# Attention and a token and channel mixer on one core: new durations and waits in the planner that sets the order

## The chip, the cores and the metric

The kernel runs on one core of a Trainium2 chip. The metric is the device time of one launch in microseconds (us); lower is better. TensorE (PE) multiplies matrices, with its weight loads shown apart as PEld; VectorE (DVE), ScalarE (ACT) and GpSimd (POOL) do the elementwise work, and SyncE (SP) issues the DMA transfers.

## The reference, cut to what matters

```python
def _attn_ref(q, k, v):                       # 8 x 8 heads, 576 rows, 64 columns
    scores = (1.0 / np.sqrt(D)) * np.matmul(q, k.transpose(0, 1, 3, 2))
    mask = pos[:, None] // 64 >= pos[None, :] // 64
    scores = np.where(mask, scores, -1000000000.0)
    attn = np.exp(scores - np.max(scores, axis=-1, keepdims=True))
    attn = attn / (np.sum(attn, axis=-1, keepdims=True) + 1e-09)
    return np.matmul(attn, v).astype(np.float32)

def _moe_ref(x, U, V, w_ch1, w_ch2):          # x: 8 x 576 x 512, the heads side by side
    h = x.transpose(0, 2, 1) @ U @ V          # U 576 x 32, V 32 x 576
    u = x + h.transpose(0, 2, 1)
    ch = np.maximum(u @ w_ch1, 0.0) @ w_ch2   # w_ch1 512 x 2048, w_ch2 2048 x 512
    return (u + ch).astype(np.float32)
```

The four matrices arrive as 64 bit words, and the kernel makes single precision numbers of them itself.

## The kernel before, in words

The work is cut into some 6500 tasks, each on one engine. `add(engine, ns, prio, fn, reads, writes, ...)` writes down a task with the nanoseconds that it is taken to occupy its engine, a priority (lower goes first) and the buffers that it reads and writes. `Plan.issue` then runs a list schedule in the build: each engine, when it is free by these nanoseconds, takes the ready task of the lowest priority number, and `fn` writes its instructions down. So the durations are never waited for on the chip. They set only the order of each engine's instructions, which the chip then executes strictly in that order, each one waiting on semaphores for what it needs. Buffers of a pool (PSUM banks) are handed out in that same run.

Three tables hold the waits between engines. After a task ends, `TAIL[e]` passes before its result leaves engine `e`, and `INTO[x]` more before a task on engine `x` can use it; `NEAR` is the wait on the same engine and `DL` that of a transfer. DVE tasks marked `port=True` and all POOL tasks are never planned at the same time.

```python
TAIL = {"PE": 165, "DVE": 78, "ACT": 105, "POOL": 20, "SP": 0}
INTO = {"PE": 355, "DVE": 35, "ACT": 35, "POOL": 310, "SP": 60}
```

The stages, in the order of time in the profile:

- Attention, 64 heads, to about 700 us. For a head: scores (L1185 for the first 12 heads, L1189 and L1190 after), maxima `mx` on DVE (L1203), exponentials `p` on ACT (L1214), reciprocals `rv` on DVE (L1230, L1231), normalising on POOL (L1240), transposes on PE (L1273), copies to `ph` on ACT (L1250) and the remainder `pl` on DVE (L1292, L1299), the product with V (L1316 for the first 10 heads, L1332 after), its two halves joined over `tmp` on ACT (L1338) and `xt` on DVE (L1340). After each second head `mix` multiplies with U and V (PE L1358, L1372, L1387; ACT L1361 `xh`, L1375 `tb`, L1377; DVE L1363 `xl`, L1376 `tz`, L1392 `ut`).
- Preparing the channel matrices beside it. A block of 128 x 512 numbers is fetched into `st` and made single precision: ACT L359, POOL L362, DVE L338, L343 and L351 (which writes `wr`), then its largest value by DVE L387. When a set of blocks is there, `power` finds a power of two (DVE L397, PE L401, DVE L407, PE L421, DVE L423), and each block is split in a high and a low half of 16 bits, ACT L455 and DVE L459. There are four such sets for the first half of the hidden width: `w1` block 0, `w2` block 0, `w1` block 1, `w2` block 1. With the last goes `agree` (DVE L482 to L488, tile `joint`), after which `level` multiplies the first four rows of `w2` again (four ACT instructions, L499).
- The first half of the channel mixer, `ffn_chunk`, in 16 chunks of 288 tokens: up products (PE L631), ACT L636 and DVE L639, down products (PE L656), DVE L668. Their PE tasks have the highest priority numbers (1e6 and up), so that PE takes them when nothing of the attention is ready. Tasks of chunks 0 and 1 come in two turns, since the second `w1` and `w2` blocks arrive late: until the second `w2` block is split, PE has only the up products of the second turn.
- The blocks of the second half of `w1` are prepared in the same manner at priority 9e5, below everything of the attention, and those of `w2` after it.
- From 834 us on, the second half of the hidden width, by a seven product scheme (PE L873).

PE, DVE, ACT and POOL each see one queue. What stands ahead in a queue and waits holds back what is behind it, whatever its priority.

Of the kernel before, what the change touches and what calls it, by code (L numbers as in the profile page):

```python
# [34 lines left out]

STAGES1 = (
# [17 lines left out]
INTO = {"PE": 355, "DVE": 35, "ACT": 35, "POOL": 310, "SP": 60}  # L54
# [86 lines left out]
class Plan:  # L141
# [105 lines left out]
def _dve(n):  # L247
    return 69 + 1.042 * n
# [13 lines left out]
def attention_then_mixer(  # L262
# [60 lines left out]
    def split64(fetches, shape, hi, lo, dst, prio, gate=(), part=slice(None), whole=None):  # L323
# [32 lines left out]
        if len(shape) > 2:  # L356
# [4 lines left out]
            "POOL", 250 + 0.85 * n, prio,  # L361
# [3 lines left out]
        add("DVE", 130 + 0.55 * n, prio, shift, [st, zt], [zt], port=True)  # L365
        add("DVE", 100 + 1.15 * n, prio, put_upper, [st, zt], [zt], port=True)
# [23 lines left out]
    def power(mu, n, by, sc, prio, pool):  # L390
# [5 lines left out]
            "DVE", 150, prio,  # L396
# [39 lines left out]
    def weights_of(half_bufs, hi, lo, blocks, scale, prio, limit=None):  # L436
# [15 lines left out]
        for n, b in enumerate(half_bufs["out"]):  # L452
            add(
                "ACT", _act(CW, True) + 90, last,
                lambda n=n: nc.scalar.activation(hi(n), raw[:, n, :], AF.Copy, scale=scale[:, 0:1]), [x[n], scale], [b],  # L455
            )
            add(
                "DVE", 150 + 1.3 * CW, last,
                lambda n=n: nc.vector.scalar_tensor_tensor(  # L459
                    out=lo(n), in0=raw[:, n, :], scalar=scale[:, 0:1], in1=hi(n), op0=ALU.mult, op1=ALU.subtract  # L460
                ),
                [x[n], scale, b], [b], port=True,
            )
# [10 lines left out]
    def agree(prio):  # L474
# [15 lines left out]
        add("DVE", 500, prio, limits, [a, b, c], [d, joint])  # L490
        add("DVE", 200, prio, ratio, [a, b, c, d], [joint])

    def level(w, bufs):

        for x in ("w2h", "w2l"):
            for k in range(0, FH, 2):
                add(
                    "ACT", _act(2 * CW, True), -1.0,
                    lambda x=x, k=k: nc.scalar.activation(w()[x][:, k : k + 2, :], w()[x][:, k : k + 2, :], AF.Copy, scale=joint[:, 0:1]),  # L499
                    [joint], bufs["w2"][k : k + 2],  # L500
                )
# [76 lines left out]
    def ffn_chunk(c, w, wb, fr=range(FC), turn=0):  # L578
# [12 lines left out]
        for k in range(KC):  # L591
            uh, ul = uh_r[k], ul_r[k]
            if not b:
                add(
                    "ACT", _act(T, True), E,
# [3 lines left out]
                    "DVE", _dve(T), E,  # L599
# [5 lines left out]
            else:  # L605
                us = take(us_r, "us")
                add(
                    "POOL", 250 + 0.85 * T, E,
# [6 lines left out]
                add("POOL", 780, E, lambda us=us, h=uh, l=ul: nc.gpsimd.tensor_sub(l.ap, us.ap, h.ap), [us, uh], [ul])  # L615
# [64 lines left out]
    def block_products():  # L680
# [115 lines left out]
        def piece(x, sc):  # L796
# [3 lines left out]
            if sc is None:  # L800
# [28 lines left out]
        def copied(out, x, iv=None):  # L829
            if iv is None:  # L830
# [3 lines left out]
                "ACT", _act(2 * T), E, lambda: nc.scalar.activation(out[0](), x[0](), AF.Copy, scale=iv.ap), [x[1], iv], [out[1]]  # L834
# [325 lines left out]
    def softmax(h, tiles, pr):  # L1160
# [37 lines left out]
        else:  # L1198
            add("PE", _pe(*ns, m=ms) + 40, pr, products, [q1, k1, q2, k2], [bank])
# [24 lines left out]
    def normalise(h, tiles, pr):  # L1224
# [9 lines left out]
        for i in tiles:  # L1234
# [4 lines left out]
                "POOL", 250 + 0.85 * w, pr,  # L1239
# [12 lines left out]
    def transpose(h, g, part, pr):  # L1252
# [41 lines left out]
        if m < n:  # L1294
# [3 lines left out]
                "DVE", _dve(64), pr,  # L1298
# [3 lines left out]
    def apply_v(h, g, pr):  # L1302
# [6 lines left out]
        if h < FP:  # L1309
# [11 lines left out]
            add("PE", cost + 15, pr, whole_products, [vr, *pt.parts], [bank], hold=[xb])  # L1321
# [15 lines left out]
        add("PE", cost + 80, pr, products, [vs, *ph.parts, *pl.parts], [bank], hold=[xb, tmp])  # L1337
        add("ACT", _act(n), pr, lambda: nc.scalar.copy(tmp[0:64, :n], bank[64:P, :n]), [bank], [tmp])  # L1338
# [5 lines left out]
    def mix(p, pr):  # L1344
# [3 lines left out]
        for rows, js in ((P, range(4)), (64, range(4, 5))):  # L1348
# [6 lines left out]
            def products(view=view, js=js, rows=rows):  # L1355
# [7 lines left out]
                "DVE", _dve(n * P), pr, lambda hi=hi, lo=lo, view=view: nc.vector.tensor_sub(lo, view(), f32(hi)),  # L1363
# [11 lines left out]
        add("ACT", _act(P), pr, lambda: nc.scalar.copy(tb.ap, low[R : 2 * R, 0:P]), [bank], [tb])  # L1375
        add("DVE", _dve(P), pr, lambda: nc.vector.tensor_add(tz.ap, low[0:R, 0:P], tb.ap), [bank, tb], [tz])  # L1376
# [126 lines left out]
```

## Time and profile before

| what | value |
|---|---|
| three runs | 1168.57, 1167.81, 1168.48 us; median 1168.48 |
| the profiled execution | 1168.67 us, of which the span from the first to the last instruction is 1166.9 us |
| busy share of the span | PE 97%, PEld 80%, DVE 82%, ACT 68%, POOL 45% |
| granted clock of PE, mean | 0.993 |
| chain that ended last | PE 70%, DVE 13%, ACT 12%, issue 3% |

The page of the profile gives the busy time of each engine, then the span in 40 equal slices with a digit for the busy tenths of each engine and the granted clock of PE, the groups of instructions by line, and the chain of work that ended last. A row of a timeline has its start, its length, the engine, the line and the tiles, and behind it in brackets the idle time before it and the instruction that ended it. A view of stretches gives the busy time of each engine between two times, with the count of its instructions.

### The profile page before, as it was taken

How to read it: one execution, taken by the hardware profiler on the slowest of the kernel's cores; microseconds unless marked ns; L12 is line 12 of the kernel's file. 1: busy time of each engine (PE TensorE's matmuls, PEld its weight loads, DVE VectorE, ACT ScalarE, POOL GpSimd, SP SyncE). 2: the span in 40 equal slices, each digit the busy share in tenths (PEclk: the TensorE clock that was granted, in tenths of full speed). 3: DMA queues.
4: the chain of work that ended last, by engine and by line, in shares of the span. 5: the costliest groups of instructions: out<-in, count | busy, mean ns of one | idle time of the engine just before them, and what ended most of it. 6: DMA issues, size and time to landing. Idle time of an engine off the chain costs nothing.

```text
span 1166.9 us, 25406 instructions
## 1 busy us (share of the span) xinstructions
PE 1135.2 (97%) x9044; PEld 934.4 (80%) x9044; DVE 958.3 (82%) x2129; ACT 794.0 (68%) x1936; POOL 524.2 (45%) x696
## 2 busy tenths in 40 slices
PE   9999997999999999999999999999999999999998
PEld 7777776877888888888888887777777777777777
DVE  6899998889887878787878773372599999999998
ACT  7878887887898888888788954325345455554543
POOL 5445554876767685858576736737200000000000
PEclk9999997999999999999999999999999999999999
DMA  5454552735443434434433312241303422331321
GB/s 142 135 146 128 152 165 83 210 114 145 119 125 103 116 105 118 110 105 114 115 101 102 94 47 72 88 134 51 102 32 92 122 62 62 122 112 34 101 82 41
DMA packets 75885, 122.70 MB, mean 105 GB/s; under 512 B 8944, under 2 KB 52976, under 8 KB 75760
## 3 DMA queue, kind: packets, MB, share of 16 engines
q1 hardware_dynamic: 75760, 121.09, 36.4%
q8 instruction: 71, 1.16, 0.4%
q14 instruction: 54, 0.44, 0.1%
HBM read 76.23 MB, written 29.49 MB: 91 GB/s over the span
## 4 chain that ended last, share of the span: by engine, by line
PE 70%; DVE 13%; ACT 12%; issue 3%; POOL 1%; DMA 0%; SPq 0%; ACTq 0%; DVEq 0%; POOLq 0%
PE bb L873 28%; PE bf L656 9%; PE bf L631 8%; PE ba L1273 5%; ACT p L1214 5%; PE ba L1332 4%; PE bg L656 3%; PE bg L631 3%; DVE mx L1203 3%; DVE pl L1292 2%; PE ba L1316 2%; PE ba L1189 1%; ACT ph L1250 1%; PE ba L1190 1%; DVE xt L1340 1%
## 5 line engine op out<-in xcount | busy, mean ns | idle before, releaser
L1240 POOL TENSOR_SCALAR p<-p,rv 128x576 f32<-128x576 f32 (+4 forms) x320 | 170.6, 548 | 125.9 <-DVE rv L1231 91.6
L1273 PE MATMUL ba<-ident,p 128*128 128x128 f32 x768 | 123.1, 276 | 7.0 <-ACT p L1214 2.2
L1214 ACT ACTIVATE p<-ba,mx 128x448 f32<-128x448 f32 (+3 forms) x248 | 114.5, 465 | 22.3 <-DVE mx L1203 17.7
L1292 DVE TENSOR_TENSOR pl<-ba,ph 128x512 fp32r<-128x512 f32 x216 | 113.7, 550 | 14.8 <-ACT ph L1250 12.6
L656 PEld LDWEIGHTS <-w2h 128*128 128x128 f16 x1024 | 100.5, 98 | 29.7 <-issue 3.7
L873 PE MATMUL bb<-hh,w1l 128*128 128x288 f16 x448 | 118.9, 286 | 0.0
L873 PE MATMUL bb<-hh,w2h 128*128 128x288 f16 x448 | 118.9, 286 | 0.0
L873 PE MATMUL bb<-hh,w2l 128*128 128x288 f16 x448 | 118.9, 286 | 0.0
L873 PE MATMUL bb<-hh,w1h 128*128 128x288 f16 x448 | 118.9, 286 | 0.0
L656 PE MATMUL bf<-hh,w2h 128*128 128x288 f16 x408 | 118.2, 290 | 0.4 <-DVE ot L668 0.4
L631 PEld LDWEIGHTS <-w1h 128*128 128x128 f16 x1024 | 97.6, 98 | 25.5 <-issue 1.7
L656 PE MATMUL bf<-hl,w2h 128*128 128x288 f16 x408 | 117.3, 288 | 0.0
L656 PE MATMUL bf<-hh,w2l 128*128 128x288 f16 x408 | 117.3, 288 | 0.0
L801 ACT CAST hh<-hb 128x576 f16<-128x576 f32 x96 | 63.6, 666 | 66.8 <-DVE hb L827 43.0
L873 PEld LDWEIGHTS <-w1h 128*128 128x128 f16 x896 | 87.7, 98 | 22.0
L873 PEld LDWEIGHTS <-w2h 128*128 128x128 f16 x896 | 87.7, 98 | 22.0
L1250 ACT CAST ph<-ba 128x512 fp32r<-128x512 f32 x216 | 98.6, 493 | 9.6 <-PE ba L1273 8.1
L1273 PEld LDWEIGHTS ba<-ident,p 128*128 128x128 f32 x768 | 90.1, 142 | 13.7 <-issue 7.8
L1203 DVE TENSOR_REDUCE mx<-ba 128x1 f32<-128x448 f32 (+3 forms) x248 | 94.1, 405 | 4.7 <-PE ba L1190 3.2
L1332 PE MATMUL ba<-ph,vs 128*128 128x256 f32 (+3 forms) x432 | 93.2, 272 | 1.8 <-DVE pl L1292 1.5
L873 PE MATMUL bb<-hl,w2h 128*128 128x288 f16 x448 | 91.6, 286 | 0.0
L873 PE MATMUL bb<-hl,w1h 128*128 128x288 f16 x448 | 91.6, 286 | 0.0
(193 smaller groups left out, 3197.0 us busy)
## 6 DMA issues: line engine op xcount, KB each, us to landing
raw<-in_qk_dram SPq DMA_DIRECT2D x63, 288.0 KB, 3.9
st<-in_w_dram SPq DMA_DIRECT2D x32, 512.0 KB, 3.8
o_d<-ot SPq DMA_DIRECT2D x72, 144.0 KB, 1.8
vr<-in_v_dram SPq DMA_DIRECT2D x32, 320.0 KB, 3.8
ur<-u_d SPq DMA_DIRECT2D x64, 144.0 KB, 2.5
wr<-o_d SPq DMA_DIRECT2D x32, 288.0 KB, 3.1
out_dram<-wr SPq DMA_DIRECT2D x31, 288.0 KB, 2.3
ur<-u_d SPq DMA_DIRECT2D x30, 288.0 KB, 3.2
```

The costliest lines, as they stand in the source:

```text
L631: nc.tensor.matmul(ps[:, :T], w()[wn][:, k, fs], m[k].ap, start=(i == 0), stop=(i == len(ops) - 1))
L656: nc.tensor.matmul(ps[:, :T], w()[wn][:, f, ms], hs[f][x].ap, start=(i == 0), stop=(i == len(ops) - 1))
L801: add("ACT", _act(2 * T, True), E, lambda: nc.scalar.copy(h.ap, x[0]()), [x[1]], [h])
L873: nc.tensor.matmul(bank[:, i, :T], x()[:, w(k)], p.ap[:, k, :], start=first and n == 0, stop=last and n == len(ops) - 1)
L1203: lambda i=i, at=at: nc.vector.tensor_reduce(out=mx[: P if i else 64, i : i + 1], in_=view(i, at), op=ALU.max, axis=AX.XY if wide else AX. ...
L1214: nc.scalar.activation(out.rearrange("p (j k) -> p j k", j=2) if wide else out, view(i, at), AF.Exp, bias=mx[:rows, i : i + 1], accum_out= ...
L1240: lambda x=x, rows=rows, i=i: nc.gpsimd.tensor_scalar(out=x, in0=x, scalar1=rv[:rows, i : i + 1], scalar2=1.0, op0=ALU.mult, op1=ALU.mult),
L1250: add("ACT", _act(n), pr, lambda: nc.scalar.copy(out(), inp()), reads, writes)
L1273: nc.tensor.transpose(out=bank[:, a : a + P], in_=pt_r[i][h % PB[i]][:, j * P : (j + 1) * P], identity=perm.ap)
L1292: "DVE", _dve(m), pr, lambda: nc.vector.tensor_sub(pl[:, low], bank[:, :m], f32(ph[:, low])), [bank, bh], [bl]
L1316: nc.tensor.matmul(bank[:, a:n], vr[:, x : x + 2, :], pt[:, _at(g, j)], start=(j == 0), stop=(j == NK[g] - 1))
L1332: nc.tensor.matmul(bank[0 : c.stop, a:n], vs[:, j, c], x[:, _at(g, j)], start=(i == 0), stop=(i == len(ops) - 1))
```

## The change

Durations in the calls of `add` and the table `INTO` are replaced, and each duration is multiplied by a factor between 0.98 and 1.02 that depends on the task's number. No task is added or removed, and no priority, buffer or dependency is changed. What each instruction computes stays the same.

```diff
+VARIANT = 6
...
-INTO = {"PE": 355, "DVE": 35, "ACT": 35, "POOL": 310, "SP": 60}
+INTO = {"PE": 355, "DVE": 60, "ACT": 60, "POOL": 200, "SP": 60}
...
         n = len(self.tasks)
+        ns *= 1 + 0.04 * ((n * 40503 + 7919 * VARIANT) % 65536 / 65536 - 0.5)
...
-            "POOL", 250 + 0.85 * n, prio,
+            "POOL", 145 + 0.85 * n, prio,
...
-        add("DVE", 130 + 0.55 * n, prio, shift, [st, zt], [zt], port=True)
-        add("DVE", 100 + 1.15 * n, prio, put_upper, [st, zt], [zt], port=True)
+        add("DVE", 50 + 0.55 * n, prio, shift, [st, zt], [zt], port=True)
+        add("DVE", 13 + 1.15 * n, prio, put_upper, [st, zt], [zt], port=True)
...
-                "DVE", 150 + 1.3 * CW, last,
+                "DVE", 1.3 * CW, last,
...
-        add("DVE", 500, prio, limits, [a, b, c], [d, joint])
+        add("DVE", 1700, prio, limits, [a, b, c], [d, joint])
...
-                    "ACT", _act(2 * CW, True), -1.0,
+                    "ACT", _act(2 * CW, True) + 100, -1.0,
...
-                "POOL", 250 + 0.85 * w, pr,
+                "POOL", 235 + 0.85 * w, pr,
...
-        add("ACT", _act(n), pr, lambda: nc.scalar.copy(tmp[0:64, :n], bank[64:P, :n]), [bank], [tmp])
+        add("ACT", _act(n) + 125, pr, lambda: nc.scalar.copy(tmp[0:64, :n], bank[64:P, :n]), [bank], [tmp])
```

Some twenty more durations change in the same way: 30 to 120 ns more for small PE, ACT and DVE steps of the attention and the mixer, less for the reductions of `power` and for the POOL subtractions (60 + 2.3 n becomes 60 + 1.98 n). The new lines shift the numbering: what is L338 to L1361 in the kernel before stands 3 lines further down in the changed kernel, and what is behind that 3 or 4.

The orders differ almost everywhere up to about 700 us, on all engines, and hardly after 834 us: there PE's, ACT's and POOL's orders are the same. Two places show what moves.

The first place is ACT, around 190 us in the profile, where the second `w2` block is split (L455, in the changed kernel L458) and `level` runs (L499, now L502). `tb`, `tmp` and `xh` belong to the mixer and to the attention. Before:

```order
L1361 CAST xh_200<-ba_98 64x128
L455 ACTIVATE w2h_245<-wr,sc 128x512
L499 ACTIVATE w2h_245<-w2h_245,joint 128x1024 x2
L499 ACTIVATE w2l_246<-w2l_246,joint 128x1024 x2
L1375 COPY tb_204<-ba_98 32x128
L455 ACTIVATE w2h_245<-wr,sc 128x512 x2
L1377 CAST t_0_202<-tz_203 32x128
L455 ACTIVATE w2h_245<-wr,sc 128x512
```

And now:

```order
L1253 CAST ph_192<-ba_97 128x320
L458 ACTIVATE w2h_245<-wr,sc 128x512
L1253 CAST ph_192<-ba_96 128x256
L458 ACTIVATE w2h_245<-wr,sc 128x512 x2
L502 ACTIVATE w2h_245<-w2h_245,joint 128x1024 x2
L502 ACTIVATE w2l_246<-w2l_246,joint 128x1024 x2
L1341 COPY tmp_196<-ba_95 64x256
L1341 COPY tmp_197<-ba_97 64x320
L458 ACTIVATE w2h_245<-wr,sc 128x512
```

Three of the four high halves now stand ahead of the four multiplications of `level`, where one did; and two `tmp` copies of the attention stand behind these, in the place of `tb`.

On DVE at the same place, the low halves (L459, now L462) stood behind the mixer's `xl`, `xh` and `tz` and steps of the next blocks. Before:

```order
L488 SCALAR_TENSOR_TENSOR joint<-joint,sc 128x1
L1363 TENSOR_TENSOR xh_200<-ba_98,xh_200 64x128
L428 SCALAR_TENSOR_TENSOR iv<-sc 128x1
L1292 TENSOR_TENSOR pl_194<-ba_96,ph_192 128x256
L428 SCALAR_TENSOR_TENSOR iv<-sc,iv 128x1
L459 SCALAR_TENSOR_TENSOR w2l_246<-wr,sc,w2h_245 128x512
L1203 TENSOR_REDUCE mx_189<-ba_95 128x1
L338 TENSOR_SCALAR z_102<-z_102 128x512
L338 TENSOR_SCALAR z_103<-z_103 128x512
```

And now:

```order
L1302 TENSOR_TENSOR ph_193<-ba_95,ph_193 64x64
L1295 TENSOR_TENSOR pl_194<-ba_97,ph_192 128x320
L1295 TENSOR_TENSOR pl_194<-ba_96,ph_192 128x256
L490 SCALAR_TENSOR_TENSOR joint<-sc 128x1
L491 SCALAR_TENSOR_TENSOR joint<-joint,sc 128x1
L462 SCALAR_TENSOR_TENSOR w2l_246<-wr,sc,w2h_245 128x512 x3
L431 SCALAR_TENSOR_TENSOR iv<-sc 128x1
L1233 TENSOR_REDUCE rv_190<-ss_164 128x2
```

Three low halves now follow each other behind `joint`. The second of them, which the first down product of the second turn needs, was the 389th task of DVE and is the 364th: 25 tasks stand behind it that stood ahead (13 on PE likewise, for that product).

The second place is DVE at about 290 us, where blocks of the second half of `w1` are prepared (L338, L343, L351; now L341, L346, L354). Before, the row with `wr` is that of the sixth of these eight blocks:

```order
L1340 TENSOR_TENSOR xt_199<-ba_96,tmp_197 64x320
L1292 TENSOR_TENSOR pl_195<-ba_97,ph_193 128x512
L1292 TENSOR_TENSOR pl_195<-ba_98,ph_193 128x448
L1292 TENSOR_TENSOR pl_194<-ba_95,ph_192 128x256
L1299 TENSOR_TENSOR ph_193<-ba_98,ph_193 64x64
L1292 TENSOR_TENSOR pl_194<-ba_96,ph_192 128x320
L1203 TENSOR_REDUCE mx_189<-bw 128x1
L1203 TENSOR_REDUCE mx_189<-ba_95 128x1
L1363 TENSOR_TENSOR xl_201<-ba_97,xh_200 128x512
L1340 TENSOR_TENSOR xt_198<-ba_98,tmp_196 64x256
L351 SCALAR_TENSOR_TENSOR wr<-st_101,z_103 128x512
```

Now the same number of rows, counted from the start of the queue, holds the last two of the eight:

```order
L1295 TENSOR_TENSOR pl_194<-ba_98,ph_192 128x320
L354 SCALAR_TENSOR_TENSOR wr<-st_100,z_102 128x512
L1343 TENSOR_TENSOR xt_199<-ba_96,tmp_196 64x256
L1206 TENSOR_REDUCE mx_188<-ba_97 128x1
L1343 TENSOR_TENSOR xt_199<-ba_95,tmp_197 64x320
L346 SCALAR_TENSOR_TENSOR z_103<-st_101,z_103 128x512
L642 SCALAR_TENSOR_TENSOR hl<-bf_90,hh 128x288
L1206 TENSOR_REDUCE mx_188<-ba_98 128x1
L1206 TENSOR_REDUCE mx_188<-ba_98 64x1
L1295 TENSOR_TENSOR pl_195<-ba_96,ph_193 128x512
L354 SCALAR_TENSOR_TENSOR wr<-st_101,z_103 128x512
```

So the blocks come up to 65 tasks earlier in DVE's queue, and the attention's steps there correspondingly later.

More of the change, by code (lines that the diff above doesn't have):

```diff
@@ L395, in power @@
         add(
-            "DVE", 150, prio,
+            "DVE", 65, prio,
             lambda: nc.vector.tensor_reduce(out=one.ap, in_=mu[:, 0:n], op=ALU.max, axis=AX.X), mu.parts[:n], [one],
@@ L426, in multiply @@
         add(
-            "DVE", 150, prio,
+            "DVE", 70, prio,
             lambda: nc.vector.scalar_tensor_tensor(
@@ L594, in ffn_chunk @@
                 add(
-                    "ACT", _act(T, True), E,
+                    "ACT", _act(T, True) + 94, E,
                     lambda u=ur[k], h=uh: nc.scalar.activation(h.ap, u.ap, AF.Copy, scale=su[:, 0:1]), [ur[k], su], [uh],
@@ L598, in ffn_chunk @@
                 add(
-                    "DVE", _dve(T), E,
+                    "DVE", _dve(T) + 60, E,
                     lambda u=ur[k], h=uh, l=ul: nc.vector.scalar_tensor_tensor(
@@ L607, in ffn_chunk @@
                 add(
-                    "POOL", 250 + 0.85 * T, E,
+                    "POOL", 235 + 0.85 * T, E,
                     lambda u=ur[k], us=us: nc.gpsimd.tensor_scalar(
@@ L730, in weights @@
                 add(
-                    "ACT", _act(1024, True), L,
+                    "ACT", _act(1024, True) + 105, L,
                     lambda b=b: nc.scalar.activation(w(b), w(b), AF.Copy, scale=sc[:, 0:1]), [sc], [b],
@@ L833, in copied @@
             add(
-                "ACT", _act(2 * T), E, lambda: nc.scalar.activation(out[0](), x[0](), AF.Copy, scale=iv.ap), [x[1], iv], [out[1]]
+                "ACT", _act(2 * T) + 105, E, lambda: nc.scalar.activation(out[0](), x[0](), AF.Copy, scale=iv.ap), [x[1], iv], [out[1]]
             )
@@ L1198, in softmax @@
         else:
-            add("PE", _pe(*ns, m=ms) + 40, pr, products, [q1, k1, q2, k2], [bank])
+            add("PE", _pe(*ns, m=ms) + (90 if wide else 50), pr, products, [q1, k1, q2, k2], [bank])
         for i, at in parts:
@@ L1297, in transpose @@
             add(
-                "DVE", _dve(64), pr,
+                "DVE", _dve(64) + 112, pr,
                 lambda: nc.vector.tensor_sub(ph[64:P, end], bank[0:64, m:n], f32(ph[0:64, end])), [bank, bh], [bh],
@@ L1336, in apply_v @@
         cost = _pe(*(n - max(P * j - q0, 0) for *_, j in ops), m=[c.stop for _, c, _ in ops])
-        add("PE", cost + 80, pr, products, [vs, *ph.parts, *pl.parts], [bank], hold=[xb, tmp])
-        add("ACT", _act(n), pr, lambda: nc.scalar.copy(tmp[0:64, :n], bank[64:P, :n]), [bank], [tmp])
+        add("PE", cost + 110, pr, products, [vs, *ph.parts, *pl.parts], [bank], hold=[xb, tmp])
+        add("ACT", _act(n) + 125, pr, lambda: nc.scalar.copy(tmp[0:64, :n], bank[64:P, :n]), [bank], [tmp])
         add(
@@ L1362, in mix @@
             add(
-                "DVE", _dve(n * P), pr, lambda hi=hi, lo=lo, view=view: nc.vector.tensor_sub(lo, view(), f32(hi)),
+                "DVE", _dve(n * P) + (112 if rows == 64 else 0), pr,
+                lambda hi=hi, lo=lo, view=view: nc.vector.tensor_sub(lo, view(), f32(hi)),
                 [bank, xh], [xl, xh] if rows == 64 else [xl],
@@ L1374, in mix @@
         add("PE", 590, pr, down, [xh, xl, *ust.parts], [bank], hold=[t3, tz, tb])
-        add("ACT", _act(P), pr, lambda: nc.scalar.copy(tb.ap, low[R : 2 * R, 0:P]), [bank], [tb])
+        add("ACT", _act(P) + 120, pr, lambda: nc.scalar.copy(tb.ap, low[R : 2 * R, 0:P]), [bank], [tb])
         add("DVE", _dve(P), pr, lambda: nc.vector.tensor_add(tz.ap, low[0:R, 0:P], tb.ap), [bank, tb], [tz])
         add("ACT", _act(P, True), pr, lambda: nc.scalar.copy(t3[0:R, :], tz.ap), [tz], [t3])
-        add("POOL", 360, pr, lambda: nc.gpsimd.tensor_sub(t3[R : 2 * R, :], tz.ap, f32(t3[0:R, :])), [tz, t3], [t3])
-        add("ACT", _act(P, True), pr, lambda: nc.scalar.copy(t3[2 * R :, :], tz.ap), [tz], [t3])
+        add("POOL", 545, pr, lambda: nc.gpsimd.tensor_sub(t3[R : 2 * R, :], tz.ap, f32(t3[0:R, :])), [tz, t3], [t3])
+        add("ACT", _act(P, True) + 120, pr, lambda: nc.scalar.copy(t3[2 * R :, :], tz.ap), [tz], [t3])
         for c in range(CPB):
```

10 lines of the change are left out of this document (5 added, 5 removed).

## The prediction

> **What bounds the kernel now.** I read the page first, for the engine that is busy and the places where it is not.
>
> ```profile
> span 1166.9 us, 25406 instructions
> PE 1135.2 (97%) x9044; PEld 934.4 (80%) x9044; DVE 958.3 (82%) x2129; ACT 794.0 (68%) x1936; POOL 524.2 (45%) x696
> PE   9999997999999999999999999999999999999998
> PEclk9999997999999999999999999999999999999999
> ```
>
> PE is busy 97% of the span, and a new order takes no matmul away: only PE's idle time and its slow clock can change, 1166.9 - 1135.2 = 31.7 us of the one, of which some at the end is fixed. The seventh slice (175 to 204 us) alone has PE and its clock at 7 tenths. Next I cut the span where the stages change: at 76 us, at the first matmul behind the late second `w2` block (198.26), at a product with V near 298 us, at the end of the attention and at the last matmul.
>
> ```profile
> core 0: us, PE busy (x) PEld busy (x) DVE busy (x) ACT busy (x) POOL busy (x), PEclk, DMA share, GB/s
> 0.00:76.00 76.00, 72.35 (x410) 58.80 (x411) 59.97 (x176) 59.20 (x167) 36.45 (x71) 1.00 0.47 133
> 76.00:198.26 122.26, 108.96 (x785) 88.27 (x783) 115.77 (x295) 99.96 (x257) 62.61 (x85) 0.94 0.51 145
> 198.26:298.19 99.93, 95.67 (x781) 80.34 (x780) 88.33 (x216) 82.28 (x226) 71.31 (x96) 0.98 0.49 141
> 298.19:330.00 31.81, 31.81 (x267) 27.14 (x265) 28.17 (x81) 25.44 (x72) 26.33 (x35) 1.00 0.53 150
> 330.00:705.00 375.00, 367.75 (x3074) 314.65 (x3073) 292.69 (x788) 314.46 (x880) 252.17 (x350) 1.00 0.37 101
> 705.00:1163.63 458.63, 458.63 (x3739) 365.21 (x3736) 372.82 (x577) 212.66 (x339) 75.37 (x64) 1.00 0.28 82
> 1163.63:1167.00 3.37, 0.00 (x0) 0.00 (x0) 0.52 (x1) 0.00 (x0) 0.00 (x0) 1.00 0.40 138
> ```
>
> PE's idle time is 3.7, 13.3, 4.3, 0, 7.3, 0 and 3.4 us. From 705 us on PE never waits. From 76 to 198 us the bound is another: DVE is busy 115.77 of 122.26 us, 95%, and PE waits for it. What PE waits for by name:
>
> ```profile
> PE ba L1273 <- DVE xt L1340: 3.3, 5, 2.0
> PE ba L1273 <- DVE tz L1376: 2.9, 3, 1.7
> PE ba L1316 <- ACT pw L1250: 2.5, 1, 2.5
> PE ba L1332 <- DVE pl L1292: 1.5, 1, 1.5
> ```
>
> Each of these is one long wait (the last column) and little beside. The stretches of 3.41 us around them show what the wait does to the clock:
>
> ```profile
> 85.48:88.90 3.42, 1.32 (x12) 1.08 (x10) 3.34 (x9) 3.40 (x9) 2.41 (x5) 1.00 0.35 91
> 88.90:92.31 3.41, 2.98 (x7) 2.44 (x8) 3.38 (x6) 2.60 (x7) 1.50 (x3) 0.50 0.00 0
> 181.06:184.47 3.41, 1.59 (x12) 1.35 (x12) 3.34 (x7) 2.84 (x8) 2.48 (x5) 1.00 0.19 35
> 184.47:187.89 3.42, 3.02 (x13) 2.06 (x14) 2.70 (x9) 2.07 (x6) 2.09 (x2) 0.50 0.86 253
> 187.89:191.30 3.41, 2.20 (x9) 1.33 (x7) 2.98 (x13) 2.61 (x6) 1.98 (x3) 0.50 0.54 134
> 191.30:194.71 3.41, 2.96 (x19) 2.96 (x20) 3.31 (x13) 2.78 (x4) 0.00 (x0) 0.50 0.00 0
> 194.71:198.13 3.42, 1.69 (x15) 1.49 (x15) 2.63 (x5) 3.40 (x7) 0.00 (x0) 1.00 0.00 0
> 198.13:201.54 3.41, 3.41 (x17) 2.36 (x15) 2.87 (x6) 3.31 (x9) 2.28 (x2) 0.50 0.00 0
> ```
>
> Three times PE is busy for less than half of such a stretch (1.32, 1.59, 1.69 us), and each time the next stretch runs at half the clock, five stretches in all. A wait is paid twice where PE has work.
>
> **The change, part by part.** It removes and adds no instruction; the cost is in the waits alone. I go by stage.
>
> *To 76 us.* PE idles 3.7 us, the start included. The order moves there by a few places and no wait is named above. I take 0, with 1 us either way.
>
> *The second `w2` block, 76 to 206 us.* In front of the first down product stands this:
>
> ```profile
> 190.70 0.72 ACT L455 ACTIVATE w2h<-wr,sc 128x512 f16<-128x512 f32 x1
> 192.05 2.19 ACT L499 ACTIVATE w2h<-w2h,joint 128x1024 f16<-128x1024 f16 x2 [0.63 <-DVE joint L488]
> 194.15 2.17 ACT L499 ACTIVATE w2l<-w2l,joint 128x1024 f16<-128x1024 f16 x2
> 196.35 0.26 ACT L1375 COPY tb<-ba 32x128 f32<-32x128 f32 x1
> 196.51 1.33 ACT L455 ACTIVATE w2h<-wr,sc 128x512 f16<-128x512 f32 x2
> 197.52 2.06 DVE L459 SCALAR_TENSOR_TENSOR w2l<-wr,sc,w2h 128x512 f16<-128x512 f32 x3
> 197.74 0.73 PE L1273 MATMUL ba<-ident,p 128*128 128x128 f32 x4 [1.73 <-DVE tz L1376]
> 198.26 0.45 PE L656 MATMUL bf<-hh,w2h 128*128 128x288 f16 x1
> ```
>
> Four `level` instructions (4.3 us of ACT) stand ahead of two of the high halves and of `tb`. So the second low half starts at 197.52 and the first product at 198.26, and PE idles 1.73 us for `tz`, which hangs on `tb`. In the new order the high halves go first, and 25 DVE tasks that stood ahead of the second low half stand behind it. The stretch has 115.77 us in 295 instructions, 0.39 us each, so these are about 9.8 us: the first product can start near 198.3 - 9.8 = 188.5 us, if DVE stays as busy as it is. Sixteen products of six matmuls follow, at full clock as in the first and the last of these twelve rows of two products:
>
> ```profile
> 204.42 0.30 PE L656 MATMUL bf<-hh,w2h 128*128 128x288 f16 x1
> ...
> 205.78 0.29 PE L656 MATMUL bf<-hl,w2h 128*128 128x288 f16 x1
> ```
>
> Eleven spacings in 1.36 us make 0.124 us for a matmul, 0.74 for a product and 16 x 0.74 = 12 us of work that needs nothing of the attention. They cover the 1.73 us wait and the 1.5 us wait for `pl` (3.2 us). Without the waits the slow stretches from 191.30 and 198.13 should go too, whose 2.96 and 3.41 busy us would take half (3.2 us). So the most to be had is 6.4 us. Against it stands that DVE is the bound: its work to 206 us is nearly the same in both orders, so that PE can only win what DVE idles, 6.5 us in the stretch. What was pulled forward (two blocks' steps) holds back the attention's DVE steps ahead of 188 us, and `tmp` now stands behind `level`, in the place of `tb`, with its 4.3 us. The price of a block, from DVE's groups of 100 to 200 us:
>
> ```profile
> L351 DVE SCALAR_TENSOR_TENSOR wr<-st,z 128x512 int32<-128x512 int32 x7 | 8.3, 1189 | 0.0
> L343 DVE SCALAR_TENSOR_TENSOR z<-st,z 128x512 int32<-128x512 int32 x8 | 5.9, 738 | 0.1
> L387 DVE TENSOR_REDUCE mu<-wr 128x1 f32<-128x512 f32 x7 | 4.7, 672 | 0.0
> L338 DVE TENSOR_SCALAR z<-z 128x512 int32<-128x512 int32 x8 | 3.5, 454 | 0.0
> ```
>
> 1.19 + 0.74 + 0.67 + 0.45 = 3.1 us. If one block's time becomes a new PE wait and nothing is won, the stage is 3.1 us longer; if all is won, 6.4 us shorter. I take half of the gain, -3.2 us, since DVE idles, but not everywhere where PE waits.
>
> *The second half of `w1`, 198 to 330 us.* Its blocks come up to 65 tasks earlier. Counted at the product with V at 298.19 us, two more blocks without their maximum (2 x 2.4 us), one maximum of twice the width (1.3 us, two of L387) and five small steps of a `power` (about 1 us, an estimate: half the mean of 0.39 us each) stand ahead of its last DVE step: 7 us more DVE work. DVE idles 99.93 - 88.33 = 11.6 us there. Where it was the bound it still idled 5%, here 5 us; that leaves 6.6 us to fill. So 0.4 us do not fit; the ends are 0 and 7 us. I take +0.5.
>
> *330 to 705 us.* PE idles 7.3 us in waits of 0.75 us and less. Nearly every task there has another place. Between the next stretches, 0 of 31.81 us and 4.3 of 99.93 us, the stage could idle from 0 to 16 us; nearest is itself. Some handoffs that were planned too short are longer now, as `tmp`'s, so that I take a tenth off, -0.7 us.
>
> *From 705 us.* PE is busy 458.63 of 458.63 us, cover enough for DVE at 372.82, and the orders of PE and ACT from 834 us are what they were. 0, and the 3.4 us after the last matmul stay.
>
> Sum: -3.2 + 0.5 - 0.7 = -3.4 us. The profiled execution took 1168.67 us, 1.8 us more than its span, and stands 0.2 us above the median of 1168.48; so 1168.67 - 3.4 = 1165.3 for it, and 1165.1 by the median.
>
> A rule that speaks against counting the slow stretches: the Trainium skill, "TensorE: Matmul & The Clock Gate", Part 1, gives a fully idle window of about 3.4 us as what halves the clock. The trace differs: the longest wait of PE is 2.5 us, and it suffices. By the rule waits of 1.5 and 1.7 us cost no clock, the most to be had before 206 us would be 3.2 us instead of 6.4 and the half of it 1.6, and the time 1166.7; by the rows it is the sum above, which I keep.
>
> **The rivals.**
>
> *No change that can be measured* (within 0.2%, 2.3 us, which is about what a measurement of this kernel tells from nothing). DVE's 95% speak for it: an order that serves the products earlier serves the attention later, the idle 13.3 us of PE before 198 us only move, and the second stage's 0.5 us are paid. Then the time is 1168.5 - 0.7 + 0.5 = 1168.3 us.
>
> *Slower.* One mechanism: the blocks of `w1` stand in DVE's queue ahead of the attention's steps between 200 and 330 us, and a step of a block that meets a POOL instruction is stretched:
>
> ```profile
> 280.21 3.09 DVE L343 SCALAR_TENSOR_TENSOR z<-st,z 128x512 int32<-128x512 int32 x1
> 281.35 1.39 POOL L1136 TENSOR_TENSOR k<-raw,k 64x576 fp32r<-64x576 f32 x1
> ```
>
> 3.09 us, where the mean of 100 to 200 us was 0.74, with POOL's L1136 beside it for the last half. The new durations of a block's steps on DVE, 13 + 1.15 x 512 = 602 ns for L343 and L351 and 50 + 0.55 x 512 = 332 ns for L338, are lower than the means above (738, 1189 and 454), so that the planner packs them tighter than the chip can run them. If the 7 us don't fit and nothing is won before, the time is 1168.5 + 7 - 0.7 = 1174.8; the sign turns when more than 3.9 + 2.3 of the 7 us are not hidden while the gain stays, or 3 us without it. Against it speaks PE's reserve of products, which are now there ten us earlier.
>
> *A larger gain*: all 6.4 us before 206, and 3 of the 7.3 us after 330, with 0.5 paid: 1168.5 - 8.9 = 1159.6. For it speaks that the planner's durations come from a trace; against it that DVE must then not idle at all.
>
> **How the numbers follow.** The forecast (2.3 to 6 us faster) gets 0.36, the larger gain 0.10, no change 0.31, slower 0.23. So faster 0.46, same 0.31, slower 0.23, and 1165.1 us. The range leaves out the far end of the larger gain and of the slower case, 1160 to 1172.5; the forecast's own is 1162.5 to 1166.1.
>
> **What would show it.** Right: the first L656 with the second `w2` block near 188 us, no half clock behind 191 us, PE idle by 206 us of 14 instead of some 17 us, and 4 to 5 us between 198 and 298. Wrong: PE waits for `pl` or `xt` above 1 us between 140 and 185 us, or above 5 us in sum from 200 to 330 us; DVE rows L346 above 2 us with PE idle behind them; or a PE idle share from 330 to 705 us that has risen above 2%.

## The result and the profile after

The changed kernel takes 1147.41 us (median of four runs, 1147.28 to 1148.27) against 1168.53 us for the kernel before beside it (1167.81 to 1170.72): a ratio of 0.982, 95% interval 0.980 to 0.984. It is 21.1 us faster; 3.4 us were forecast, and the range ended at 1160.0. The profiled execution took 1147.53 us, its span is 1145.7 us.

The head of the page after, as it was shown of before:

```profile
span 1145.7 us, 25439 instructions
PE 1123.0 (98%) x9044; PEld 931.3 (81%) x9044; DVE 954.8 (83%) x2129; ACT 791.7 (69%) x1936; POOL 524.5 (46%) x696
PE   9989998999999999999999999999999999999998
PEclk9999999999999999999999999999999999999999
```

The span is 21.2 us shorter, and the same 9044 matmuls keep PE busy for 1123.0 us instead of 1135.2. So 12.2 us of the gain lie in time that the page calls busy, and 9.0 us in idle time (31.7 to 22.7 us). To see where, equal stretches of both kernels are set side by side, in the columns of the prediction's stretches. Before:

```profile
76.00:206.00 130.00, 116.70 (x834) 94.00 (x832) 121.69 (x308) 105.83 (x271) 66.22 (x87) 0.93 0.49 140
206.00:330.00 124.00, 119.74 (x996) 101.76 (x996) 110.59 (x282) 101.84 (x283) 94.03 (x128) 1.00 0.52 148
330.00:690.00 360.00, 352.75 (x2943) 301.82 (x2942) 285.08 (x771) 306.70 (x861) 249.81 (x346) 1.00 0.38 105
```

After:

```profile
0.00:76.00 76.00, 71.05 (x413) 58.62 (x414) 62.93 (x182) 60.51 (x169) 38.61 (x72) 1.00 0.48 141
76.00:206.00 130.00, 120.73 (x903) 97.51 (x902) 124.59 (x323) 107.56 (x280) 70.35 (x94) 0.99 0.53 156
206.00:330.00 124.00, 121.31 (x1018) 104.07 (x1017) 108.96 (x283) 110.10 (x298) 94.42 (x126) 1.00 0.48 136
330.00:690.00 360.00, 357.89 (x3035) 311.32 (x3034) 283.44 (x767) 301.50 (x855) 248.82 (x347) 1.00 0.37 103
```

The first count in each row is PE's matmuls. From 76 to 330 us PE runs 91 more than before (903 + 1018 against 834 + 996), and from 330 to 690 us another 92 (3035 against 2943). At 360 / 3035 = 0.119 us each, these 92 are 10.9 us, half of the gain; the stretch from 76 to 330 us is the other half (below). Of the 10.9 us only 5.1 were idle time of PE (7.25 to 2.11 us). The rest is in the busy time: 352.75 / 2943 = 0.1199 us a matmul before, 357.89 / 3035 = 0.1179 after, with the clock at 1.00 in both.

From 76 to 330 us PE's idle time fell from 17.6 to 12.0 us, and its time at half clock from five stretches of 3.41 us to one, beginning at 180.91 us. The five held 14.57 us of busy time by the rows of the prediction (2.98, 3.02, 2.20, 2.96, 3.41); half of it is the price, 7.3 us, and the one left costs 1.7. So 5.6 us are idle time and 5.6 us (7.3 less 1.7) the clock, 11.2 together.

The second `w2` block is where the forecast put its gain. Some of PE's rows there, after:

```profile
179.82 0.47 PE L1335 MATMUL ba<-ph,vs 128*128 128x256 f32 x2 [2.95 <-DVE ph L1302]
...
182.92 0.46 PE L659 MATMUL bf<-hh,w2h 128*128 128x288 f16 x1
...
184.35 0.29 PE L659 MATMUL bf<-hh,w2h 128*128 128x288 f16 x1
```

The first down product of the second turn stands at 182.92 us (198.26 before; 188.5 forecast). What remains is one wait of 2.95 us, now for `ph`, and the half clock behind it: the product at 182.92 takes 0.46 us, that at 184.35 the full clock's 0.29. The stretches around it:

```profile
177.49:180.91 3.42, 1.09 (x10) 1.09 (x11) 3.27 (x11) 1.78 (x4) 0.69 (x1) 1.00 0.63 155
180.91:184.32 3.41, 3.41 (x18) 2.79 (x17) 3.38 (x12) 3.35 (x4) 0.95 (x2) 0.50 0.00 0
```

DVE is busy 3.27 of 3.42 us while PE waits: here DVE is still the bound.

Of one experiment (without the factor and without the mixer's durations) a disturbed execution at a mean clock of 0.849 is left out, so that its time stands on one run.

### The profile page after: what moved, and what is told of

Same layout as the page of the kernel before. It is cut to its first block, busy times and chain, and to the rows that moved or that the text cites. A ratio compares the mean times of both kernels' runs of the same rounds, so it can differ in the third digit from the quotient of the medians.

```text
span 1145.7 us, 25439 instructions
## 1 busy us (share of the span) xinstructions
PE 1123.0 (98%) x9044; PEld 931.3 (81%) x9044; DVE 954.8 (83%) x2129; ACT 791.7 (69%) x1936; POOL 524.5 (46%) x696
## 4 chain that ended last, share of the span: by engine, by line
PE 72%; DVE 14%; ACT 8%; issue 3%; POOL 2%; DMA 1%; SPq 0%; ACTq 0%; DVEq 0%; POOLq 0%
PE bb L876 29%; PE bf L659 10%; PE bf L634 8%; PE ba L1276 6%; PE ba L1335 5%; ACT p L1217 3%; PE bg L634 3%; DVE mx L1206 3%; DVE pl L1295 2%; PE bg L659 2%; PE ba L1319 1%; PE ba L1192 1%; PE ba L1193 1%; PE ba L1376 1%; DVE hl L642 1%
## 5 line engine op out<-in xcount | busy, mean ns | idle before, releaser
L1243 POOL TENSOR_SCALAR p<-p,rv 128x576 f32<-128x576 f32 (+4 forms) x320 | 172.9, 555 | 125.6 <-DVE rv L1234 73.4
L1253 ACT CAST ph<-ba 128x512 fp32r<-128x512 f32 x216 | 99.1, 492 | 12.0 <-PE ba L1276 10.9
```

The source lines that it names most:

```text
L1243: lambda x=x, rows=rows, i=i: nc.gpsimd.tensor_scalar(out=x, in0=x, scalar1=rv[:rows, i : i + 1], scalar2=1.0, op0=ALU.mult, op1=ALU.mult),
L1253: add("ACT", _act(n), pr, lambda: nc.scalar.copy(out(), inp()), reads, writes)
```

## The experiments

Two questions were put: is it the new numbers or the draw of the factor; and which numbers make the steady state's gain. The theories, by the letters of the expectations: A, numbers nearer to the chip's make the gain, the draw only scatters it. B, most of it is the luck of the draw. C, the waits of `INTO` alone make it. T, of the durations it is that of the `tmp` copies (L1338). M, it is the mixer's `tb`, `t` on POOL and last `t`.

The expectations speak of gains by stage. These are worked out from the trace: for each of PE's tasks the time from its start to the next one's, less the 10th percentile for its kind, summed over the tasks that lay in that stage before. The same tasks are compared each time. The count of matmuls from 330 to 690 us in the table is a plainer measure of the same and agrees with it: (3047 - 2943) x 0.119 = 12.4 us for the largest, where the sum gives 11.7. Negative is faster. The time at half clock leaves out the end of the kernel, where it is in nearly all.

The ratio is to the kernel before as it was timed beside each experiment (1167.8 to 1170.6 us). The four columns behind it come from one profiled execution each, which need not be the median one: the factor alone was profiled at 1170.6 us, with a median of 1174.7 and runs up to 1177.9, and e18 at 1166.0 with a median of 1169.6. A small gain by stage is not told from a new order by itself: the factor alone, which brings no better number, already gives 2.3 us from 330 to 705 us.

| kernel | median us | ratio, 95% interval | 76 to 330 us | 330 to 705 us | matmuls 330 to 690 | half clock us |
|---|---|---|---|---|---|---|
| before | 1168.5 | | | | 2943 | 17.1 |
| the change | 1147.4 | 0.982 (0.980 to 0.984) | -10.9 | -10.7 | 3035 | 3.4 |
| e1 no factor | 1148.4 | 0.983 (0.979 to 0.987) | -8.0 | -11.7 | 3047 | 6.8 |
| e2 factor alone | 1174.7 | 1.005 (1.003 to 1.007) | +4.9 | -2.3 | 2967 | 17.1 |
| e3 `INTO` alone | 1160.4 | 0.993 (0.990 to 0.996) | -3.6 | -4.4 | 2980 | 6.8 |
| e4 factor, draw 1 | 1156.4 | 0.990 (0.986 to 0.994) | -2.0 | -11.1 | 3038 | 17.1 |
| e5 durations alone | 1157.4 | 0.991 (0.988 to 0.993) | -3.8 | -7.0 | 3006 | 6.8 |
| e6 `INTO`, POOL only | 1173.3 | 1.004 (1.002 to 1.006) | +5.1 | -2.7 | 2968 | 17.1 |
| e7 `INTO`, ACT | 1159.2 | 0.992 (0.989 to 0.995) | +2.1 | -11.2 | 3038 | 17.1 |
| e8 `INTO`, PE | 1171.9 | 1.002 (1.000 to 1.004) | +6.1 | -1.3 | 2951 | 20.5 |
| e9 `INTO`, mixer | 1160.7 | 0.992 (0.989 to 0.995) | -4.4 | -3.7 | 2976 | 10.2 |
| e10 `INTO`, `tmp` | 1155.1 | 0.987 (0.984 to 0.990) | -3.4 | -10.2 | 3031 | 6.8 |
| e11 `INTO`, ACT, DVE | 1155.8 | 0.988 (0.982 to 0.994) | -6.2 | -10.7 | 3041 | 10.2 |
| e12 mixer undone | 1159.2 | 0.991 (0.988 to 0.994) | -2.3 | -5.9 | 3000 | 10.2 |
| e13 `tmp` undone | 1159.5 | 0.991 (0.988 to 0.995) | -6.3 | -0.8 | 2952 | 13.7 |
| e14 no factor, mixer undone | 1153.9 | one run | -6.1 | -8.2 | 3014 | 10.2 |
| e15 factor, draw 2 | 1154.7 | 0.989 (0.984 to 0.993) | -1.4 | -11.1 | 3034 | 6.8 |
| e16 factor, draw 3 | 1150.7 | 0.985 (0.981 to 0.989) | -7.1 | -9.2 | 3022 | 3.4 |
| e17 `tmp` alone | 1162.0 | 0.995 (0.993 to 0.996) | -3.2 | -3.2 | 2969 | 10.2 |
| e18 `INTO`, ACT without `tmp` | 1169.6 | 1.002 (1.001 to 1.003) | +3.9 | -5.4 | 2990 | 13.7 |

### The factor and its draw: e1, e2, e4, e15, e16

The change without the factor (e1); the factor alone on the kernel before (e2); the change with another `VARIANT` (e4, e15, e16):

```diff
# e1, against the changed kernel
-        ns *= 1 + 0.04 * ((n * 40503 + 7919 * VARIANT) % 65536 / 65536 - 0.5)
# e2, against the kernel before
+VARIANT = 6
+        ns *= 1 + 0.04 * ((n * 40503 + 7919 * VARIANT) % 65536 / 65536 - 0.5)
# e4; e15 with 2, e16 with 3
-VARIANT = 6
+VARIANT = 1
```

> All new durations and the new waits (INTO), each duration as it is, without the factor between 0.98 and 1.02. Theory A (the numbers nearer to the chip give the gain, 1168.5 to 1147.4 us): 1144 to 1151 us. Theory B (the order before was one draw of many and the change drew a better one; the numbers' being right has no part in it): anywhere from 1147 to 1172 us. Theory C (the waits between engines alone): as A.

> The old durations and waits with the factor alone, drawn as in the change. Theory A: no gain beyond the spread of such draws, 1164 to 1173 us. Theory B: a spread of 10 us and more, so about as likely below 1160 us as above. Theory C: as A.

> The change with another draw of the factor (VARIANT 1 for 6), so every task's duration is off by another share within 2%. Theory A: 1144 to 1152 us, and the orders differ nearly everywhere all the same. Theory B: 1150 to 1172 us, since the good draw is lost. Theory C: as A.

> The change with another draw of the same factor (VARIANT 2). Theory A (durations and waits nearer the chip's make the gain, the draw only scatters it): from 330 to 705 us a gain of 9 to 12 us as with the draws 6 and 1 and without the factor (10.7, 11.1, 11.7), and from 76 to 330 us anything between a gain of 11 and a loss of 6; time 1146 to 1160 us. Rival B (the draw 6 is picked and most of the gain is luck): the gain from 330 to 705 us falls below 6 us as well and the time is above 1158.

> The change with a third draw (VARIANT 3). As for draw 2: theory A gives 9 to 12 us of gain from 330 to 705 us, anything from -11 to +6 us before it and a time of 1146 to 1160 us; rival B less than 6 us there and a time above 1158.

The row of 330 to 690 us without the factor:

```profile
330.00:690.00 360.00, 358.02 (x3047) 311.30 (x3045) 284.46 (x767) 301.06 (x853) 247.79 (x345) 1.00 0.37 103
```

With draw 1:

```profile
330.00:690.00 360.00, 357.99 (x3038) 311.23 (x3036) 285.68 (x777) 306.13 (x864) 246.83 (x341) 1.00 0.37 105
```

With and without the factor, and with four draws of it, the steady state runs 3022 to 3047 matmuls, where the kernel before runs 2943 and the factor alone gives 2967. So from 330 us on the new numbers make the gain whatever the draw, as A says; that they make it because they are nearer to the chip's is checked for one of them only (`tmp`, below). Before 330 us the five kernels with all the new numbers gain 10.9, 8.0, 2.0, 1.4 and 7.1 us: the order of that stretch is a matter of the draw, and 2% on a duration moves it by 9 us. Their times are 1147.4, 1148.4, 1156.4, 1154.7 and 1150.7 us, in the mean 1151.5: B is right for some 4 of the 21 us, draw 6 being the best of the five, and no more. Two of A's times were missed: the factor alone lies above its 1164 to 1173 us, and draw 1 lies above its 1144 to 1152 us, where only B's range held. The factor alone shows that a reshuffle can also lose: its PE waits from 76 to 330 us begin with

```profile
PE ba L1276 <- DVE xt L1343: 4.1, 3, 2.9
PE ba L1390 <- ACT p L1217: 3.5, 2, 2.8
PE ba L404 <- DVE xt L1343: 2.3, 1, 2.3
```

(us in total, times, the longest): long single waits with half clock behind them.

### Waits or durations: e3, e5, e6

```diff
# e3, against the kernel before; e6 with the old 35 for DVE and ACT
-INTO = {"PE": 355, "DVE": 35, "ACT": 35, "POOL": 310, "SP": 60}
+INTO = {"PE": 355, "DVE": 60, "ACT": 60, "POOL": 200, "SP": 60}
# e5: all new durations, the old INTO, no factor
```

> The table INTO alone (ACT and DVE 35 to 60, POOL 310 to 200), old durations, no factor. Theory A with the durations as the main part: 1160 to 1170 us, a third of the gain at most. Theory B: anywhere from 1147 to 1172 us. Theory C: 1146 to 1152 us, nearly the whole gain.

> All new durations, the old INTO, no factor. So far: durations and waits without factor 1148.4 us, waits alone 1160.4. If the two parts add up, the durations alone give the other 12 us: 1155 to 1159 us, with the gain from 330 to 705 us (some 7 us) and less of the 8 us from 76 to 198 us. If the waits are what makes it all and the durations only shift the draw: 1165 us and more. If each alone gives most: 1148 to 1152.

> Of INTO only POOL's entry (310 to 200), ACT and DVE stay at 35. If the earlier POOL steps are the cause of what the waits alone gave (8.7 us): 1158 to 1162 us. If the later steps of ACT and DVE (35 to 60) are: 1165 to 1171 us.

The waits alone gain 4.4 us from 330 to 705 us, the durations alone 7.0, both (e1) 11.7: they add up, and C covers less than half. The entry of POOL alone gains 2.7 us there, which the factor alone nearly does too, and it loses 5.1 before that stage. At 1173.3 us it lies above both times that were expected. So the 8 us that the waits bring in all are not POOL's entry by itself; the 25 ns of DVE and ACT were not tried alone, and no run shows that the new waits are nearer to the chip's own than the old.

### Which durations: e7, e8, e9, e10, e11, e12

All but the last are the kernel before with the new `INTO` and some of the new durations; the last is the changed kernel with three durations undone. Of e9 and e10 only the new lines are shown.

```diff
# e7: all of ACT's; e11: all of ACT's and DVE's
# e8: PE's
-            add("PE", _pe(*ns, m=ms) + 40, pr, products, [q1, k1, q2, k2], [bank])
+            add("PE", _pe(*ns, m=ms) + (90 if wide else 50), pr, products, [q1, k1, q2, k2], [bank])
...
-        add("PE", cost + 80, pr, products, [vs, *ph.parts, *pl.parts], [bank], hold=[xb, tmp])
+        add("PE", cost + 110, pr, products, [vs, *ph.parts, *pl.parts], [bank], hold=[xb, tmp])
# e9: the mixer's; e12 undoes these in the changed kernel
+        add("ACT", _act(P) + 120, pr, lambda: nc.scalar.copy(tb.ap, low[R : 2 * R, 0:P]), [bank], [tb])
+        add("POOL", 545, pr, lambda: nc.gpsimd.tensor_sub(t3[R : 2 * R, :], tz.ap, f32(t3[0:R, :])), [tz, t3], [t3])
+        add("ACT", _act(P, True) + 120, pr, lambda: nc.scalar.copy(t3[2 * R :, :], tz.ap), [tz], [t3])
# e10: tmp's
+        add("ACT", _act(n) + 125, pr, lambda: nc.scalar.copy(tmp[0:64, :n], bank[64:P, :n]), [bank], [tmp])
```

> The new INTO and the new durations of ACT's tasks alone (tmp, tb, t, level and the first halves: 94 to 125 ns more). If the longer ACT steps are what the steady state from 330 to 705 us needed: 1150 to 1155 us, with that stage as in the change. If it is PE's or DVE's: 1158 to 1163 us.

> The new INTO and the new durations of PE's tasks alone (10 to 100 ns more for scores and products with V). If PE's durations are what the steady state needed, as PE is the bound there and every start that is planned too early is a wait in its queue: 1150 to 1155 us. If it is ACT's or DVE's: 1158 to 1163 us.

> The new INTO and three new durations, those of the mixer's short chain tb (ACT L1375), t (POOL L1378) and the last t (ACT L1379). In the steady state (the PE tasks that lay from 330 to 705 us before) PE lost 10.7 us less in the change, 4.4 less with the waits alone, 11.2 less with waits and all ACT durations; 5.2 us of what it lost before were waits of L1387 for the last t. Theory M (this chain was planned too short): 8 us or more of the 10.7 there. Theory T (the tmp copies, 108 of them, are the main part): 4 to 6 us there. The whole time is left to the draw in the earlier stretch: 1150 to 1165 us.

> The new INTO and the new duration of tmp (ACT L1338, 125 ns more, 108 times) alone. Theory M: 4 to 6 us less lost in the steady state, as with the waits alone. Theory T: 8 us or more. The whole time 1150 to 1165 us.

> The new INTO and the new durations of ACT and of DVE (limits 1700 for 500, the blocks' steps shorter, small remainders longer). If DVE's right numbers are what the stage of the weight blocks (76 to 330 us) needed: 8 us or more less lost there, as in the change (10.9) and without the factor (8.0), and with the steady state of 11 us some 1149 us in all. If that stage is a matter of the draw: between 0 and 10 us there, 1149 to 1160 us.

> The whole change, the factor included, with the old durations of tb, t and the last t. Theory M: 4 us or more are lost again in the steady state. Theory T: under 2 us are. The draw changes as well, so the whole time may be anywhere from 1147 to 1160 us.

In the steady state ACT's durations with the waits give all of the gain (e7: 11.2 us, 3038 matmuls), PE's add nothing to the waits (e8: 1.3), and of ACT's the one of `tmp` is nearly enough (e10: 10.2). The row of 330 to 690 us with the waits alone, and then with the waits and `tmp`:

```profile
330.00:690.00 360.00, 354.40 (x2980) 305.50 (x2978) 282.76 (x772) 304.52 (x858) 248.24 (x343) 1.00 0.38 104
330.00:690.00 360.00, 356.42 (x3031) 310.93 (x3030) 284.64 (x771) 302.96 (x856) 245.01 (x340) 1.00 0.38 104
```

The mixer's three do not (e9: 3.7, no more than the waits), so M falls as the cause by itself. But the change without them loses 4.8 us (e12), as M expected, and T alone does not give that. e7 shows how little the steady state says of the whole: with the same 11 us there it is 12 us slower than the change, since the stretch before 330 us lost 2.1 us and its half clock stayed at 17.1 us. By its time, 1159.2 us, it would have spoken for PE or DVE as the cause, and e8, at 1171.9, lies above both ranges that were put down for it. DVE's durations beside ACT's (e11) did not bring the 8 us before 330 us that were expected if they were what that stage needed, but 6.2, which a draw also gives.

### Is tmp needed, and is it enough: e13, e14, e17, e18

```diff
# e13, against the changed kernel
-        add("ACT", _act(n) + 125, pr, lambda: nc.scalar.copy(tmp[0:64, :n], bank[64:P, :n]), [bank], [tmp])
+        add("ACT", _act(n), pr, lambda: nc.scalar.copy(tmp[0:64, :n], bank[64:P, :n]), [bank], [tmp])
# e14: e12 without the factor
# e17: the kernel before with + 125 for tmp, and nothing else
# e18: e7 without + 125 for tmp
```

> The change with one duration undone: the tmp copies (L1341) are planned at the old 0.29 us instead of 0.42. Theory T (the tmp copies make the steady state's gain): of the 10.7 us that the change gains from 330 to 705 us at least 6 are lost there, the gain is 5 us or less, and the time is near 1153 us or above. Rival S (the gain is made of many durations and no single one is needed): the stretch keeps 8 us or more, and the time differs from 1147.4 us only by what the stretch of 76 to 330 us does.

> The change without the factor, and with the durations of the mixer's tb, t on POOL and last t undone. It repeats the experiment in which undoing them lost 4.8 us of 10.7 from 330 to 705 us, without the factor that lay over it. If the mixer's durations are needed, the stretch gains 7 us or less (against 11.7 without the factor alone) and the time is near 1153 us; if that loss was the draw of the factor, it gains 10 us or more and the time is near 1149 us.

> The kernel before with one edit: tmp (L1338) is planned 125 ns longer; the table INTO and all else are the old ones. The same edit with the new INTO gained 10.2 us from 330 to 705 us, and the new INTO alone 4.4. Theory T (tmp's duration by itself): a gain of 7 us or more there, time 1155 to 1162 us. Rival W (it needs the new waits, since a longer tmp and a longer wait behind it are the same delay planned twice): 4 us or less there, time near 1165 us.

> The kernel before with the new INTO and all new durations of ACT except tmp's. With tmp's they gained 11.2 us from 330 to 705 us; the new INTO alone gained 4.4. Theory T: no more than the waits alone, 5 us or less there, time near 1163 us. Rival S (the gain is made by many durations of ACT together): 8 us or more there, time near 1159 us.

The row of the change with `tmp` undone:

```profile
330.00:690.00 360.00, 352.71 (x2952) 305.28 (x2951) 286.35 (x771) 301.81 (x858) 246.59 (x342) 1.00 0.37 103
```

2952 matmuls, 9 more than before the change: with every other new number in place, 9.9 of the 10.7 us are lost. Of these 4.3 us are one wait of 2.6 us and half a stretch at half clock behind it (last section), which may be this order's bad luck; the other 5.6 agree with what `tmp` is worth in two more places, 5.8 us on top of the waits (10.2 in e10 less 4.4 in e3) and 5.8 on top of ACT's other durations (11.2 in e7 less 5.4 in e18). So `tmp` is needed. It is not enough: alone it gives 3.2 us (e17), hardly more than the factor alone, the waits alone 4.4, the two 10.2. T's expectation of 7 us or more for it alone fell, and that of its rival held; T holds with the waits beside it (e18's 5.4 us are just over the 5 that T allowed there, and its time is 6 us above the one expected). Whether 125 ns is the right amount, or any delay of these copies would do, was not tried. Undoing the mixer's durations costs 3.5 us there without the factor (e14: 8.2 against 11.7, between the 7 and the 10 that were to decide). They may be a smaller second part, but this stays open: e10 has the old ones too and still gains 10.2, and the draws alone spread by 2.5 us.

Why `tmp`? In the kernel before, its group from 330 to 690 us reads

```profile
L1338 ACT COPY tmp<-ba 64x256 f32<-64x256 f32 x70 | 27.0, 396 | 11.9 <-PE ba L1332 10.7
```

70 copies of 396 ns. The planner took 52 + 0.833 n, 265 and 319 ns for 256 and 320 columns, 292 in the mean, so that the plan was short of ACT time by 0.104 us with each copy, 7.3 us over the stretch; 125 ns more make 417. The longest of PE's waits there, before (us in total, times, the longest):

```profile
PE ba L1273 <- ACT p L1214: 2.2, 6, 0.5
PE ba L1387 <- ACT p L1214: 0.9, 2, 0.7
PE ba L1387 <- DVE xt L1340: 0.5, 1, 0.5
PE ba L1387 <- ACT t L1379: 0.4, 1, 0.4
PE ba L1273 <- DVE xt L1340: 0.3, 2, 0.2
PE ba L1189 <- ACT p L1214: 0.3, 1, 0.3
```

And after:

```profile
PE ba L1391 <- ACT p L1217: 0.4, 2, 0.3
PE ba L1276 <- ACT p L1217: 0.3, 1, 0.3
```

The mixer's product with V (L1387) and the scores (L1189) read no `p`, and the transposes (L1273) read it only after POOL has normalised it: what they lack is the PSUM bank that an exponential still reads.

I set each late start of PE (over 0.12 us) against the last of its inputs and the last reader of the bank that the planner gave it. Late banks hold back 16.7 us before and 8.2 after; 8.6 with `INTO` and `tmp` (e10), 12.7 with `INTO` alone (e3) and 15.5 with `tmp` undone (e13). The largest part is `p`: 8.5 us before, 3.6 after. So by this reckoning PE loses 8.5 us less to late banks, where the stage gained 10.7.

That `p` is late because `tmp` stands ahead of it in ACT's queue is what the planned times suggest, and the runs do not bear it out: by about the same reckoning `p`'s part is about 4.4 us with `INTO` alone, 5.0 with `INTO` and `tmp`, and 5.5 with `tmp` undone. Adding `tmp` to the waits takes 4.1 us off the late banks (12.7 to 8.6) and none off `p`'s part. So it is shown that these copies' planned time matters and that late banks shrink with it; by which step it acts stays open.

## Why the prediction was wrong

The direction was right, and none of its cases held the time: even its larger gain was 1159.6 us.

**The premise.** "Only PE's idle time and its slow clock can change" is the step that failed. It took the page's busy share for work. A record of 0.29 us at a spacing of 0.124 us (the rows of L656 in the prediction) goes on for 0.17 us after the next matmul could have started, so a wait up to that length is counted as busy. In the steady state such waits were 10.9 - 5.1 = 5.8 us, as much as the idle time that was won. A lighter mix of matmuls explains little of it: at the 10th percentile of each kind's spacing, the mean for a matmul is 0.1043 us before and 0.1041 after, about 0.6 us in all.

**330 to 705 us: -0.7 was forecast, -10.7 measured.** The term was a tenth of the idle 7.3 us. Idle time fell by 5.1 us in 360, so even of that it was seven tenths, and the hidden waits come on top. The cause was named ("some handoffs that were planned too short are longer now, as `tmp`'s") and given no size. The working that was missing: 70 copies with some 0.1 us missing in the plan, 7 us, which with the new waits are worth most of the stage's gain.

**76 to 206 us: -3.2 was forecast, with -6.4 as the most.** The mechanism was right: the high halves ahead of `level`, the low halves behind each other, the products there early, and even earlier than forecast (182.92 us for 188.5). PE's idle time by 206 us is 4.95 + 9.27 = 14.2 us, as forecast, and no half clock lies behind 191 us until the kernel's end. But the clock was under-sized: the forecast counted the two last slow stretches, and four of five went, 5.6 us in place of 3.2. The "half of the gain" that was taken off for DVE's bound was too much: DVE's idle time went from 8.3 to 5.4 us of 130. The sum of the tasks that lay from 76 to 198 us fell by 7.7 us.

**198 to 330 us: +0.5 was forecast, -3.2 measured.** The added DVE work did fit: from 198 to 298 us PE idles 2.6 us, not 4 to 5.

```profile
198.00:298.00 100.00, 97.42 (x809) 82.30 (x808) 92.57 (x244) 86.47 (x239) 79.19 (x105) 1.00 0.50 146
```

DVE is busy 92.57 of 100 us, 4.2 more than in the same stretch before (88.33), where 7 were added up. The stretched block step that the slower rival was built on did not come: the twelve of L346 take 0.67 to 1.04 us, where one took 3.09 before. That rival also misread one duration: L351 keeps its 100 + 1.15 x 512 = 689 ns in the changed plan, and only L343 goes to 602. Of the signs that were to speak against the forecast one came half: a wait above 1 us between 140 and 185 us, but for `ph` and not for `pl` or `xt`, and it cost one slow stretch.

**To 76 us and from 705 us: 0 was forecast**, -0.2 and +0.5 measured.

**The chance of luck.** The forecast argued for one order. Five orders by the new numbers differ by 9 us, most of it before 330 us, so that a range of 12.5 us was too narrow for such a change even with the right mean.

**The rule on the clock.** The Trainium skill, "TensorE: Matmul & The Clock Gate", Part 1, has an idle window of about 3.4 us halve the clock. The trace still differs: behind a longest wait of 2.95 us the clock fell here too, and the slow stretches that went were worth 5.6 us, which by the rule, taken as a window without any work, would not have been there to win.

## What to carry to other kernels

Where a planner sets the order, compare each planned duration with the mean of its group in the trace, and begin with the steps that are many and planned too short: the longer plan for 70 copies that were planned at 292 ns and take 396 was, together with the new waits, nearly half of this gain. Size what an order can win by the time per matmul against the best stretch of the same kind, since a busy share of 97% still held 12 us. Where a stretch depends on the draw, build several orders and time them: 2% on the durations moved this kernel by 9 us.

## What the runs showed of the chip that was not expected

The clock is halved in the middle of the densest stage too, if PE gets one long wait. With `tmp` undone (e13):

```profile
541.02:544.43 3.41, 3.41 (x31) 3.17 (x29) 2.57 (x9) 1.20 (x4) 3.41 (x7) 1.00 0.71 219
544.43:547.85 3.42, 0.81 (x8) 0.58 (x7) 3.36 (x3) 1.52 (x4) 2.62 (x3) 1.00 0.30 71
547.85:551.26 3.41, 3.41 (x17) 2.89 (x16) 2.43 (x6) 0.96 (x2) 0.00 (x0) 0.50 0.46 135
```

The wait was this:

```profile
PE ba L1276 <- DVE xt L1343: 2.6, 1, 2.6
```

PE is busy 0.81 of 3.42 us, then the clock is 0.50 and a full stretch holds 17 matmuls, where the one before the wait held 31. In the five cases shown (0.81 here, 1.09 after the change, 1.32, 1.59 and 1.69 before it) less than half of a stretch was busy, and the longest wait was 2.95 us. Half is near the border but not the border itself. In the traces of all twenty kernels, the clock falls 41 times ahead of the kernel's end. PE was busy for 0.34 to 2.04 us of the 3.41 us just before, in 35 of the cases for less than half. Of two stretches that were hardly under half busy, 1.64 us in e5 (from 187.47 us) and 1.65 in e2 (from 257.79 us), neither was followed by half clock. When the clock comes back is not settled: a busy time of 2.96 us at half clock was followed by full clock, one of 3.02 us was not.
